# Operand addresses at multiples of 64 bytes, one expert instead of two read by columns, and a held decoding step

## The chip, the cores and the metric

The kernel runs on one core of a Trainium2 chip. The metric is the device time of one execution in microseconds (us); lower is better. The core has five engines: PE (TensorE, matrix products), DVE (VectorE), ACT (ScalarE), POOL (GpSimd) and SP (SyncE, which here issues most DMAs). Each works through its own queue in order. PEld is the loading of a matmul's stationary operand, which overlaps the matmul before it.

## The reference, cut to what matters

Three layers in a chain, all float32 inputs except that the last layer's weights come as 64-bit floats:

```python
# attention: batch 4, heads 12, sequence 448, head size 64
q_n, k_n = rmsnorm(q, g_q), rmsnorm(k, g_k)
attn = softmax(q_n @ k_n.T / 8)
x = (attn @ v)                       # -> [1792 tokens, 768]
# soft mixture of experts: 8 experts with 4 slots each
logits = x @ phi                     # [1792, 32]
slot_input = softmax(logits, over tokens).T @ x
slot_out[e] = relu(slot_input[e] @ w1[e]) @ w2[e]   # w1 768x1024, w2 1024x768
x = softmax(logits, over slots) @ slot_out
# feed forward
h = x @ w_in                         # 768 x 2048
g = h * sigmoid(1.702 * h)
out = g @ w_out                      # 2048 x 768
```

## The kernel before, in words

The work stands in three stretches of the span.

**Attention** (0 to about 300 us) runs over 24 pairs of heads with f16 scores; all engines take part. Its queues are written by a planner: each step is recorded with an engine, a cost, a due time and its needs, and `run()` sorts the steps of each engine into one order. The table `HOLD` adds needs to named steps.

**The experts** (about 300 to 394 us). 48 MB of expert weights stream in on SP's queue in a fixed order. For expert e, `first_half` (L1186) multiplies the slots by w1, `hidden_turn` (L1214 to L1218) transposes the hidden values through PE, and `second_half` (L1225) multiplies them by w2, whose rows arrive in pieces of 768 KB. For the last two experts (`EL = NE - 2`) w2 is not read in rows but in columns: `piece()` (L120) reads 512 or 256 of the 768 columns of 512 rows at a time, so that the last sums can start before all of it is there. Those sums are the planner's steps ("p", kk, ee): for each of six column blocks kk, `last_mm` (L1318) adds eight small matmuls of each of the two experts; ("pc", kk) copies the block on DVE (L1326), ("pt", kk) turns it on PE (L1329), ("pa", kk) adds it to `before` on DVE (L1333), and `u_step` (L1347) multiplies `before` by the first columns of w_in. While PE has nothing to do, `warm_c` (L1340) issues idle f16 matmuls into a spare tile. When all six blocks are summed, ACT copies u (L1693, called u0 below), PE makes the first hidden columns (`f_first`, L1430), ACT applies the activation (`f_hi` L1448, gh), and the first matmul into y (L1484) can run. `close()` then frees the buffers of the stage.

**The feed forward** (394 us to the end). w_out is 64-bit floats, loaded raw (`raw_w`, L1278) and decoded by ACT and DVE in steps (`decode64`, L167 to L181; steps ("wd", f, i, h)); `w_hi` (L1297, L1289) and `w_lo` (L1301) split each value into two fp32r tiles, wh and wl (named wo while they stand in one pool). The rest of w_in is loaded by `late_load` (L1369) and decoded likewise. The first 512 tokens go through `y_first` (L1484), 16 blocks f of 128 hidden columns each, three passes (hi x hi, hi x lo, lo x hi) of matmuls with 512 and 256 columns. The other 1,280 tokens go through `s_mm` (L1637): seven products instead of eight of half-size blocks, each again in three passes, every matmul a 128x128 stationary block of activations (gh, gl, sl) and 256 moving columns of weights (wo, wh, wl) or of sums of weights (th, tl), all fp32r. `f_mm` for these tokens is L1556.

**Addresses.** Tiles are laid out one after another in each of 128 partitions. The tile esc, [128, 1], takes 32 bytes and stands ahead of the large tiles on the left side; on the right side nothing stands ahead of them. By the address map of the built program the following operands of PE start at 32 bytes past a multiple of 64: lg, pacc, all of attention's rings, the weight rings wr, cT, gh, gl, gg, the ring of hs and pc, uh, ul, selu, keep, and the pairs of wo. These start at a multiple of 64: ident, wt, wi, the last eight wh and wl, th, tl, sg, sl, ust, hTz, siT and before. Of the matmuls of L1637 so 480 (wo by gh or gl, 440, and wo by sl, 40, where sl starts at a multiple) have a moving operand at 32, 741 (wh, wl, th or tl by gh or gl) have the moving operand at a multiple and the stationary one at 32, and 108 (th or wh by sl) have both at a multiple.

Of the kernel before, what the change touches and what calls it, by code (L numbers as in the profile page):

```python
# [8 lines left out]
F32 = mybir.dt.float32  # L9
# [5 lines left out]
ALU = mybir.AluOpType  # L15
# [5 lines left out]
def soft_moe_block_kernel(  # L21
# [60 lines left out]
    selw = const.tile([128, NS], F32, name="selw")  # L82
    gmax = const.tile([128, 1], F32, name="gmax")
    rgmax = const.tile([128, 1], F32, name="rgmax")
    esc = const.tile([128, 1], F32, name="esc")
    lg_t = const.tile([128, B, C, NS], F32, name="lg")
    pacc = const.tile([128, DM], F32, name="pacc")
    macc = [const.tile([128, 1], F32, name=f"macc{b}") for b in range(B)]
    zacc = const.tile([128, 1], F32, name="zacc")

    wpool_ctx = tc.tile_pool(name="wpool", bufs=NW, reuse_waits="tile")
    wpool = wpool_ctx.__enter__()

    EL = NE - 2
    order_w = [(x, e) for e in range(3) for x in ("w1", "w2")] + [("w1", 3)]
    order_w += [(x, e + d) for e in range(3, EL) for x, d in (("w1", 1), ("w2", 0))] + [("w1", NE - 1)]
    stream = [(x, e, hh) for x, e in order_w for hh in range(2)] + [("w2", EL, i) for i in range(4)]
    wt = {}  # L100
    is_kept = {}
    win64 = w_in.bitcast(U32)
# [3 lines left out]
    def place(t, kept=False, i=None, merged=False):  # L106

        if i is None:
            i = nstream[0]
            nstream[0] += 1  # L110
        kind, e, hh = key = stream[i]
        wt[key], is_kept[key] = t, kept

        def piece(n):
            if kind == "w1":
                rows = w1[e, hh * 384:hh * 384 + 384, :].rearrange("(p n) f -> p n f", n=3)
                nc.sync.dma_start(out=t[:, n * F1:(n + 1) * F1], in_=rows[:, n])
            elif e == EL:
                a, c = (0, 512, DM)[n:n + 2]
                nc.sync.dma_start(  # L120
                    out=t[:, 4 * a:4 * c].rearrange("p (f c) -> p f c", f=4),
                    in_=w2[EL + hh // 2, hh % 2 * 512:hh % 2 * 512 + 512, a:c].rearrange("(f p) c -> p f c", p=128),
                )
            else:
                r = hh * 512 + n // 2 * 256
                rows = w2[e, r:r + 256, :].rearrange("(p n) c -> p n c", n=2)
                nc.sync.dma_start(out=t[:, n * DM:(n + 1) * DM], in_=rows[:, n % 2])

        def whole(n):
            if kind == "w1":  # L130
                nc.sync.dma_start(out=t, in_=w1[e, hh * 384:hh * 384 + 384, :].rearrange("(p n) f -> p (n f)", n=3))
            else:
                r = hh * 512 + n * 256
                nc.sync.dma_start(
                    out=t[:, 2 * n * DM:2 * (n + 1) * DM], in_=w2[e, r:r + 256, :].rearrange("(p n) c -> p (n c)", n=2)
                )

        if merged and (kind == "w1" or e < EL):
            return [lambda n=n: whole(n) for n in range(1 if kind == "w1" else 2)]
        return [lambda n=n: piece(n) for n in range(3 if kind == "w1" else 4 if e < EL else 2)]  # L140

    late = []

    def load_all(t, kept=False):
        last = stream[nstream[0]][:2] == ("w2", EL)
        fs = place(t, kept, merged=True)
        if last:

            late.append(fs.pop())
        if len(late) == 4:  # L150
            fs += late
        for f in fs:
            f()

    def reload(*key):

        if is_kept[key] is not None and nstream[0] < len(stream) - (0 if is_kept[key] else 4):
            load_all(wt[key], is_kept[key])

    def decode64(dst, src, low):  # L160
# [82 lines left out]
    for i, tag in enumerate(("ssq", "y0", "nt")):  # L243
# [36 lines left out]
    HOLD = {  # L280
        ("meansq", 1): [("invert", 0, 5)], ("gain", 2): [("kn", 0)], ("square", 3): [("khi", 0)], ("q2", 0): [("khi", 0)],
        ("meansq", 2): [("qn", 0)], ("meansq", 3): [("qlo", 0)], ("lq", 1): [("v", 0)], ("e1", 2): [("tqb", 22)], ("ev", 0): [("tqb", 22)], ("ev", 1): [("tqb", 22)], ("v", 0): [("lq2", 0), ("lk2", 0)],
    }

    SHIFT = dict(
# [34 lines left out]
    def op(name, eng, dur, due, fn, needs=(), takes=None, gives=()):  # L320
        names[name] = len(ops)
        due += SHIFT.get(name if isinstance(name, str) else name[0], 0)
        ops.append((name, eng, dur, due, fn, list(needs) + HOLD.get(name, []), takes, list(gives)))
# [529 lines left out]
    def rtile(nm, shape, dt=F32):  # L853
        R[nm] = rt_p.tile(shape, dt, tag=nm, name=nm)
        return R[nm]
# [85 lines left out]
        nc.vector.tensor_copy(out=rtile("nmg", [128, 1]), in_=MS.pop("w"))  # L941

    def w_exp():
        nc.scalar.activation(out=rtile("wgt", [128, 1]), in_=macc[B - 1], func=AF.Exp, bias=R["nmg"], scale=1.0)

    def w_z():
        nc.vector.tensor_tensor(out=rtile("zs", [128, 1]), in0=R["wgt"], in1=zacc, op=ALU.mult)

    def w_sum():
        fill(9)  # L950
# [8 lines left out]
        nc.vector.reciprocal(out=rz, in_=R["zt"])  # L959

    def w_scale():
        nc.vector.tensor_scalar(out=selw, in0=sel32, scalar1=R["wgt"], scalar2=None, op0=ALU.mult)

    op("w_sel", "DVE", 0.2, 100, w_sel, [("exp", 4, 0, 0)])
    w_last = None
# [61 lines left out]
    with tc.manual_schedule():  # L1027
# [93 lines left out]
        def combine():  # L1121
            nm = bp.tile([P, B, C, 1], F32, name="nm")
            flat = lambda t: t.rearrange("p b c o -> p (b c o)")
            nc.vector.tensor_reduce(out=flat(nm), in_=lg_t.rearrange("p b c s -> p (b c) s"), axis=AX.X, op=ALU.max)
            nc.vector.tensor_tensor(out=lg_t, in0=lg_t, in1=nm.to_broadcast([P, B, C, NS]), op=ALU.subtract)
            nc.scalar.activation(out=lg_t, in_=lg_t, func=AF.Exp)
            nc.vector.tensor_reduce(out=flat(nm), in_=lg_t.rearrange("p b c s -> p (b c) s"), axis=AX.X, op=ALU.add)
            nc.vector.tensor_scalar(out=nm, in0=nm, scalar1=1e-9, scalar2=None, op0=ALU.add)
            rc = bp.tile([P, B, C, 1], F32, name="rc")
            nc.vector.reciprocal(out=flat(rc), in_=flat(nm))  # L1130
            nc.scalar.activation(out=bp.tile([128, 1], F32, name="warm"), in_=flat(rc)[:, :1], func=AF.Silu)
            nc.vector.tensor_tensor(out=lg_t, in0=lg_t, in1=rc.to_broadcast([P, B, C, NS]), op=ALU.mult)

        def combine_turn(b):
# [103 lines left out]
        for e in range(EL):  # L1238
# [1 line left out]
            hidden_turn(e)  # L1240
            first_half(e + 1, 1)
            second_half(e)
        first_half(NE - 1, 0)
        hidden_turn(EL)
        first_half(NE - 1, 1)
        sums_read()
        hidden_turn(NE - 1)
        while turns_w[1] < NWI:
            win_turn()
        w2ctx.close()  # L1250
# [57 lines left out]
            nc.scalar.activation(out=out, in_=ps[:, :3], func=AF.Copy)  # L1308
            nc.scalar.activation(out=dst[:, SF:], in_=ps[:, 3, :SH], func=AF.Copy)

        def last_mm(kk, ee):

            if ee == 0:
                st["p", kk] = ps_h.tile([128, Q1], F32, tag="h", name="h")
            for f in range(8):
                g, a, c = f % 4, *((0, 512) if kk < 4 else (512, DM))
                w = wt["w2", EL, 2 * ee + f // 4][:, 4 * a:4 * c].rearrange("p (f c) -> p f c", f=4)
                nc.tensor.matmul(  # L1318
                    st["p", kk][32 * g:32 * g + 32, :128], hTz[(EL + ee) % 2][:, f % 2, f // 2],
                    w[:, g, kk * 128 - a:kk * 128 - a + 128],  # L1320
                    start=(ee == 0 and f < 4), stop=(ee == 1 and f >= 4),
                )

        def last_copy(kk):
            st["pc", kk] = hp.tile([128, Q1], F32, tag="hs", name="pc")
            nc.vector.tensor_copy(out=st["pc", kk][:, :128], in_=st["p", kk][:, :128])  # L1326
# [346 lines left out]
        for i in range(60):  # L1673
            op(("warm", i), "PE", 0.11, IDLE, warm_c, [("warm", i - 1)] if i else [])
        for kk in range(KD):
            for ee in range(2):
                i = 2 * kk + ee
                if i < 8:
                    op(("arrive", i), "SP", (2.6 if i < 4 else 1.5) if i else 0, -1, lambda: None, [("arrive", i - 1)] if i else [])
                op(  # L1680
                    ("p", kk, ee), "PE", 0.62, kk, lambda kk=kk, ee=ee: last_mm(kk, ee),
                    [("arrive", kk // 4 * 4 + 2 * ee + 1)] + [("p", kk, 0)] * ee, None if ee else ("h", kk),
                )
            op(("pc", kk), "DVE", 0.22, kk, lambda kk=kk: last_copy(kk), [("p", kk, 1)], ("hs", kk), [("h", kk)])
            op(("pt", kk), "PE", 0.14, kk, lambda kk=kk: last_turn(kk), [("pc", kk)], None, [("hs", kk)])
            op(("pa", kk), "DVE", 0.09, kk, lambda kk=kk: last_add(kk), [("pt", kk)])
            op(
                ("u", kk), "PE", 0.5, kk + 2, lambda kk=kk: u_step(kk), [("pa", kk)] + ([("u", kk - 1)] if kk else []) + [("p", KD - 1, 1)] * (kk == KD - 2),
            )
        for b in range(B):  # L1690
            op(("cT", b), "ACT", 0.48, 1, lambda b=b: ct_copy(b))
# [32 lines left out]
        for f in range(KF):  # L1724
# [3 lines left out]
            for h in (None,) if f else (0, 1):  # L1728
                o = lambda *n, h=h: (n[0], f) + n[1:] + (() if h is None else (h,))
                n = 1 if h is None else 0.52  # L1730
                op(
                    o("raw"), "SP", 0.15 if h == 0 else 2.2 * n, f, lambda f=f, h=h: raw_w(f, h), [o("raw", h=0)] if h else [("arrive", 7)] if f < 3 else ["close"],
                    None if h else ("wr", f),
                )
                op(
# [184 lines left out]
```

## Time and profile before

| | us |
|---|---|
| median of 3 runs | 650.08 |
| lowest, highest | 648.41, 651.06 |
| the profiled execution's own time | 648.1 |
| its span in the profile | 646.3 |
| PE busy | 596.4 (92%) |
| DVE busy | 485.2 (75%) |
| ACT busy | 386.5 (60%) |

The profiled execution is 1.8 us longer than its span and 2.0 us below the median. Busy time on PE is modelled from its start times, since matmuls overlap: a matmul's duration (281 ns for 256 columns) is its passage, while the distance from one start to the next tells the rate. Shares are means over stretches with different limits, so the rows that count are those of one stretch.

### The profile page before, as it was taken

How to read it: one execution, taken by the hardware profiler on the slowest of the kernel's cores; microseconds unless marked ns; L12 is line 12 of the kernel's file. 1: busy time of each engine (PE TensorE's matmuls, PEld its weight loads, DVE VectorE, ACT ScalarE, POOL GpSimd, SP SyncE). 2: the span in 40 equal slices, each digit the busy share in tenths (PEclk: the TensorE clock that was granted, in tenths of full speed). 3: DMA queues.
4: the chain of work that ended last, by engine and by line, in shares of the span. 5: the costliest groups of instructions: out<-in, count | busy, mean ns of one | idle time of the engine just before them, and what ended most of it. 6: DMA issues, size and time to landing. Idle time of an engine off the chain costs nothing.

```text
span 646.3 us, 12124 instructions
## 1 busy us (share of the span) xinstructions
PE 596.4 (92%) x4575; PEld 399.4 (62%) x4575; DVE 485.2 (75%) x896; ACT 386.5 (60%) x768; POOL 170.3 (26%) x209
## 2 busy tenths in 40 slices
PE   2699999999999999999895788999999999999997
PEld 1333444344433443456452355887899999999997
DVE  6888979999999998546353118999999988565653
ACT  3767888877877786643333018998664545444442
POOL 3676683736774765120002000000000000000000
PEclk9999999999999999998999799999999999999999
DMA  7889999799999998956999997985120101010101
GB/s 188 294 166 225 215 190 174 168 232 208 188 222 200 179 237 202 282 190 249 409 415 419 413 374 279 333 282 192 41 97 3 50 1 50 2 50 1 51 2 50
DMA packets 143339, 121.55 MB, mean 188 GB/s; under 512 B 105232, under 2 KB 125968, under 8 KB 142000
## 3 DMA queue, kind: packets, MB, share of 16 engines
q1 hardware_dynamic: 141776, 116.41, 64.6%
q10 hardware_dynamic: 1440, 4.26, 1.7%
q8 instruction: 36, 0.59, 0.4%
q14 instruction: 23, 0.19, 0.1%
q0 software_dynamic: 64, 0.10, 0.1%
HBM read 92.18 MB, written 5.51 MB: 151 GB/s over the span
## 4 chain that ended last, share of the span: by engine, by line
PE 56%; DMA 13%; DVE 12%; ACT 7%; SPq 5%; issue 4%; POOL 2%; ACTq 0%; DVEq 0%; POOLq 0%
PE y L1637 24%; PE pv L597 5%; PE sc L578 5%; PE y L1484 5%; DVE wr L567 4%; DMA wr<-wr 3%; PE h L1186 3%; SPq L120 3%; DMA wt<-in_moe_w_dram 3%; DMA ws<-in_moe_w_in_dram 3%; DMA wr<-in_k_dram 2%; PE pv L592 2%; PE mx L562 2%; PE so_ps L1225 2%; PE f L1556 1%
## 5 line engine op out<-in xcount | busy, mean ns | idle before, releaser
L567 DVE TENSOR_REDUCE wr<-mx 128x2 f16<-128x896 f32 x92 | 99.9, 1086 | 15.9 <-PE mx L562 15.4
L582 ACT ACTIVATE e<-sc,esc 128x448 f32<-128x448 f32 x96 | 57.2, 633 | 8.2 <-PE sc L578 6.3
L1637 PE MATMUL y<-wo,gh 128*128 128x256 f32 x320 | 59.6, 281 | 0.0
L1582 ACT ACTIVATE gh<-gg 128x512 fp32r<-128x512 f32 x40 | 25.3, 631 | 56.8 <-PE y L1637 53.6
L585 POOL TENSOR_TENSOR es<-es,e 128x448 f32<-128x448 f32 x37 | 44.6, 1210 | 32.9 <-PE pv L597 22.0
L1588 DVE TENSOR_TENSOR gl<-gg,gh 128x512 fp32r<-128x512 f32 x40 | 27.6, 690 | 32.5 <-ACT gh L1582 32.3
L578 PE MATMUL sc<-wr 128*128 128x448 f16 (+1 forms) x192 | 47.6, 360 | 2.4 <-ACT e L582 2.2
L1637 PEld LDWEIGHTS y<-wo,gh 128*128 128x128 f32 x320 | 49.2, 190 | 0.0
L1637 PE MATMUL y<-wl,gh 128*128 128x256 f32 x172 | 48.4, 281 | 0.0
L1637 PE MATMUL y<-wh,gh 128*128 128x256 f32 x172 | 48.3, 281 | 0.0
L582 ACT ACTIVATE es<-sc,esc 128x448 f32<-128x448 f32 x54 | 33.5, 635 | 20.3 <-PE sc L578 20.1
L445 ACT ACTIVATE wr<-wr 128x512 f32<-128x512 f32 x48 | 30.2, 635 | 15.3 <-DVE wr L1056 4.5
L1637 PE MATMUL y<-wh,gl 128*128 128x256 f32 x138 | 38.8, 281 | 0.0
L578 PEld LDWEIGHTS <-wr 128*128 128x128 f16 (+1 forms) x256 | 19.1, 101 | 30.2 <-issue 21.6
L1563 ACT ACTIVATE gg<-f 128x512 f32<-128x512 f32 x40 | 23.8, 599 | 16.8 <-DVE gl L1588 13.8
L1637 PE MATMUL y<-wo,gl 128*128 128x256 f32 x120 | 33.9, 282 | 0.0
L450 DVE TENSOR_REDUCE wr<-wr 128x16 f32<-128x1024 f32 x24 | 29.1, 1211 | 5.7 <-ACT wr L445 5.7
L505 POOL TENSOR_TENSOR wr<-wr 128x512 f32<-128x512 f32 x26 | 30.2, 1180 | 11.8 <-DVE wr L498 7.5
L1637 PEld LDWEIGHTS y<-wh,gh 128*128 128x128 f32 x172 | 32.4, 188 | 0.0
L1637 PEld LDWEIGHTS y<-wl,gh 128*128 128x128 f32 x172 | 32.4, 188 | 0.0
L1637 PE MATMUL y<-tl,gh 128*128 128x256 f32 x111 | 31.2, 281 | 0.0
L1637 PE MATMUL y<-th,gh 128*128 128x256 f32 x111 | 31.2, 281 | 0.0
(325 smaller groups left out, 1673.4 us busy)
## 6 DMA issues: line engine op xcount, KB each, us to landing
wt<-in_moe_w_dram SPq DMA_DIRECT2D x9, 1536.0 KB, 10.2
wr<-in_moe_w_out_dram SPq DMA_DIRECT2D x15, 768.0 KB, 6.3
wt<-in_moe_w_dram SPq DMA_DIRECT2D x12, 512.0 KB, 7.8
wr<-in_moe_w_dram SPq DMA_DIRECT2D x8, 768.0 KB, 12.3
ws<-in_moe_w_in_dram SPq DMA_DIRECT2D x12, 512.0 KB, 4.8
wr<-in_moe_w_dram SPq DMA_DIRECT2D x12, 384.0 KB, 5.5
out_dram<-o SPq DMA_DIRECT2D x12, 384.0 KB, 2.4
wr<-in_k_dram SPq DMA_DIRECT2D x11, 384.0 KB, 5.3
```

The source lines that it names most:

```text
L445: nc.scalar.activation(out=sqt[p][:, 8 * i:8 * i + 8], in_=rows(p, i), func=AF.Square, scale=D ** -0.5)
L450: nc.vector.tensor_reduce(out=part(ssqt, p, 1), in_=sqt.pop(p), axis=AX.X, op=ALU.add)
L505: eng.tensor_tensor(out=n, in0=n, in1=r.to_broadcast([P, 8, D]), op=ALU.mult)
L567: nc.vector.tensor_reduce(out=lanes(of(qb_t, p), 1)[:m, h:h + n, c, 0:1], in_=MX.pop((p, g))[:m, :n, :S], axis=AX.X, op=ALU.max,)
L578: nc.tensor.matmul(out, cols(a, n, c), cols(b, n), start=first, stop=not first)
L582: nc.scalar.activation(out=E[p, h, c], in_=SC.pop((p, h, c)), func=AF.Exp, scale=esc)
L585: on(f"e{h}{c}", p)[0].tensor_tensor(out=E[p, h, 0], in0=E[p, h, 0], in1=E[p, h, c], op=ALU.add)
L597: nc.tensor.matmul(PV[p][h * D:(h + 1) * D, :], t[:, 6 * n + 3 * h + c], E[p, h, c], start=(c == 0), stop=False)
L1484: nc.tensor.matmul(Y[t, u], a[:, t * 128:(t + 1) * 128], b[:, YC[u]], start=(f == 0 and j == 0 and (u == 0 or t % 2 == 0)), stop=(f == KF ...
L1582: nc.scalar.activation(out=t, in_=src, func=AF.Copy)
L1588: nc.vector.tensor_tensor(out=t, in0=src, in1=hi.bitcast(F32), op=ALU.subtract)
L1637: nc.tensor.matmul(out, l[:, a], r, start=fresh and x == 0, stop=last and x == 2)
```

## The change

Three edits.

1. Addresses. esc moves behind the large tiles of its pool; a new pool of 32 bytes on the right edge holds wgt (before in a ring) and so moves every pool on the right by 32 bytes; a one-column tile called warm is dropped. By the address map of the changed program the operands of PE start at multiples of 64 bytes, but for sub-slices inside a few small tiles (one column of macc, the strides of selw, pacc and hs).
2. `EL = NE - 1`: only expert 7's w2 is read by columns, in two pieces of 1 MB and two of 0.5 MB. Expert 6's w2 is read in four pieces of rows and multiplied in `second_half`. A step ("p", kk) has 8 matmuls instead of 16.
3. `HOLD` makes the first decoding steps of w_out on DVE, ("wd", 0, 0, 0) and ("wd", 0, 0, 1), wait for ("pa", 5), the last sum.

```diff
@@ the tiles
-    esc = const.tile([128, 1], F32, name="esc")
     lg_t = const.tile([128, B, C, NS], F32, name="lg")
...
     zacc = const.tile([128, 1], F32, name="zacc")
+    esc = const.tile([128, 1], F32, name="esc")
+    edge = ctx.enter_context(tc.tile_pool(name="edge", bufs=1, side="right"))
+    wgt = edge.tile([128, 1], F32, name="wgt")
...
-            nc.scalar.activation(out=bp.tile([128, 1], F32, name="warm"), in_=flat(rc)[:, :1], func=AF.Silu)
+            nc.scalar.activation(out=macc[0], in_=flat(rc)[:, :1], func=AF.Silu)
@@ the last experts
-    EL = NE - 2
+    EL = NE - 1
...
-    order_w += [(x, e + d) for e in range(3, EL) for x, d in (("w1", 1), ("w2", 0))] + [("w1", NE - 1)]
-    stream = [(x, e, hh) for x, e in order_w for hh in range(2)] + [("w2", EL, i) for i in range(4)]
+    order_w += [(x, e + d) for e in range(3, EL) for x, d in (("w1", 1), ("w2", 0))]
+    stream = [(x, e, hh) for x, e in order_w for hh in range(2)] + [("w2", EL, i) for i in range(2)]
...
-                    in_=w2[EL + hh // 2, hh % 2 * 512:hh % 2 * 512 + 512, a:c].rearrange("(f p) c -> p f c", p=128),
+                    in_=w2[EL, hh * 512:hh * 512 + 512, a:c].rearrange("(f p) c -> p f c", p=128),
...
-        first_half(NE - 1, 0)
         hidden_turn(EL)
-        first_half(NE - 1, 1)
         sums_read()
-        hidden_turn(NE - 1)
...
-                    st["p", kk][32 * g:32 * g + 32, :128], hTz[(EL + ee) % 2][:, f % 2, f // 2],
+                    st["p", kk][32 * g:32 * g + 32, :128], hTz[EL % 2][:, f % 2, f // 2],
                     w[:, g, kk * 128 - a:kk * 128 - a + 128],
-                    start=(ee == 0 and f < 4), stop=(ee == 1 and f >= 4),
+                    start=(f < 4), stop=(f >= 4),
@@ the held step
     HOLD = {
...
+        ("wd", 0, 0, 0): [("pa", 5)], ("wd", 0, 0, 1): [("pa", 5)],
     }
```

The planner writes new orders from this. On DVE, at the end of the experts, the queue before (pc is a copied block of the last sums, before+= its sum, wf and wr tiles of the decoding of w_out, keep a copy of before):

```order
L1326 COPY pc<-h 128x128
L181 TENSOR_SCALAR wf<-wf 128x384
L1326 COPY pc<-h 128x128
L1333 TENSOR_TENSOR before<-t,before 128x32
L181 TENSOR_SCALAR wf<-wf 128x384
L1333 TENSOR_TENSOR before<-t,before 128x32
L167 SCALAR_TENSOR_TENSOR wf<-wr,wf 128x384 x4
L1722 COPY keep<-before 128x192
L1301 TENSOR_TENSOR wo<-wf,wo 128x384 x2
L167 SCALAR_TENSOR_TENSOR wr<-wr 128x768
```

and in the changed program (its line numbers differ by a few):

```order
L1324 COPY pc<-h 128x128
L1331 TENSOR_TENSOR before<-t,before 128x32 x2
L183 TENSOR_SCALAR wf<-wf 128x384 x2
L169 SCALAR_TENSOR_TENSOR wf<-wr,wf 128x384 x4
L1715 COPY keep<-before 128x192
L169 SCALAR_TENSOR_TENSOR wr<-wr 128x768
L1301 TENSOR_TENSOR wo<-wf,wo 128x384 x2
L169 SCALAR_TENSOR_TENSOR wf<-wf,wr 128x768
```

The two TENSOR_SCALARs moved behind the last sum, and the STT of f = 1 (wr by wr) ahead of the two subtractions of f = 0.

On ACT, at the same place, the queue before (wf by wr is the first step of a block's decoding, wr by wr the second, u the copy u0, wo the splitting, gh and gg the activation of the first hidden columns):

```order
L170 ACTIVATE wf<-wr 128x384 x2
L170 ACTIVATE wf<-wr 128x768
L1693 ACTIVATE u_3945<-u 32x256
L1297 ACTIVATE wo<-wf 128x384
L1289 ACTIVATE wo<-wf 128x384
L173 ACTIVATE wr<-wr 128x768
L1448 ACTIVATE gh<-h 128x512
L1443 ACTIVATE gg<-h 128x512
```

and in the changed program:

```order
L172 ACTIVATE wf<-wr 128x384 x2
L172 ACTIVATE wf<-wr 128x768
L175 ACTIVATE wr<-wr 128x768
L1686 ACTIVATE u_3971<-u 32x256
L1297 ACTIVATE wo<-wf 128x384
L1289 ACTIVATE wo<-wf 128x384
L172 ACTIVATE wf<-wr 128x768
L1446 ACTIVATE gh<-h 128x512
```

The second step of f = 1, wr by wr, moved ahead of u0, and the first step of f = 2 ahead of gh.

On PE, the last expert's hidden values and the sums before (h by wt,siT is L1186, so_ps `second_half`, h by wt,hTz or wr,hTz the last sums):

```order
L1186 MATMUL h<-wt,siT 32x256 x12
L1225 MATMUL so_ps<-wr,hTz_3356 32x256 x24
L1186 MATMUL h<-wt,siT 32x256 x12
L1214 MATMUL t<-ident,hs 128x128 x2
L1186 MATMUL h<-wt,siT 32x256 x12
L1207 MATMUL t<-ident,so 128x96 x2
L1214 MATMUL t<-ident,hs 128x128 x2
```

and in the changed program:

```order
L1189 MATMUL h<-wt,siT 32x256 x12
L1228 MATMUL so_ps<-wr,hTz_3359 32x256 x24
L1189 MATMUL h<-wt,siT 32x256 x12
L1217 MATMUL t<-ident,hs 128x128 x2
L1189 MATMUL h<-wt,siT 32x256 x12
L1228 MATMUL so_ps<-wt,hTz_3358 32x256 x24
L1217 MATMUL t<-ident,hs 128x128 x2
L1210 MATMUL t<-ident,so 128x96 x2
```

Expert 6's 24 matmuls by rows of w2 are new there. Behind these rows the idle matmuls go from 37 to 15, and the last sums from 96 matmuls to 48.

## Rows read from the trace of the kernel before

**Rows 1.** The page: busy time of each engine; chain that ended last, by line.

```profile
PE 596.4 (92%) x4575; PEld 399.4 (62%) x4575; DVE 485.2 (75%) x896; ACT 386.5 (60%) x768; POOL 170.3 (26%) x209
...
PE y L1637 24%; PE pv L597 5%; PE sc L578 5%; PE y L1484 5%; DVE wr L567 4%; DMA wr<-wr 3%; PE h L1186 3%; SPq L120 3%; DMA wt<-in_moe_w_dram 3%; DMA ws<-in_moe_w_in_dram 3%; DMA wr<-in_k_dram 2%; PE pv L592 2%; PE mx L562 2%; PE so_ps L1225 2%; PE f L1556 1%
```

**Rows 2.** Stretches: start:end, length, busy (count) of PE, PEld, DVE, ACT, POOL, clock, DMA.

```profile
448.20:642.24 194.04, 194.01 (x1569) 190.34 (x1565) 147.09 (x352) 96.78 (x171) 0.00 (x0) 1.00 0.09 34
...
394.70:420.00 25.30, 23.59 (x130) 20.09 (x131) 24.62 (x35) 24.26 (x39) 0.00 (x0) 1.00 0.92 326
420.00:448.20 28.20, 27.29 (x234) 23.19 (x233) 26.67 (x37) 26.19 (x42) 0.00 (x0) 1.00 0.70 240
```

**Rows 3.** Timeline of PE, a stretch with wo moving (start, us, line, tiles, count).

```profile
552.76 0.40 PE L1637 MATMUL y<-wo,gh 128*128 128x256 f32 x2
...
553.84 0.28 PE L1637 MATMUL y<-th,gh 128*128 128x256 f32 x1
```

**Rows 4.** The same, a stretch with th, tl, wh and wl moving.

```profile
541.64 0.28 PE L1637 MATMUL y<-th,gh 128*128 128x256 f32 x1
...
541.88 0.28 PE L1637 MATMUL y<-th,sl 128*128 128x256 f32 x1
...
543.76 0.40 PE L1637 MATMUL y<-wo,gh 128*128 128x256 f32 x2
```

**Rows 5.** Timeline of PE, f16 matmuls: idle ones on ident, and attention's scores.

```profile
373.85 1.80 PE L1340 MATMUL t<-ident 128*128 128x256 f16 x15 [0.28 <-DVE hTz L1218]
...
100.79 1.31 PE L578 MATMUL sc<-wr 128*128 128x448 f16 x6
```

**Rows 6.** Groups of PE from 448.2 to 642.24, shapes apart (count, busy, mean ns).

```profile
L1637 PE MATMUL y<-wo,gh 128*128 128x256 f32 x320 | 59.6, 281 | 0.0
...
L1484 PE MATMUL y<-wh,gh 128*128 128x512 f32 x24 | 6.6, 398 | 0.0
```

**Rows 7.** Timeline of all engines around the last sum and the first y.

```profile
389.05 0.36 DVE L181 TENSOR_SCALAR wf<-wf 128x384 uint32<-128x384 uint32 x1 [0.65 <-ACT wf L170]
...
390.10 1.93 PE L1347 MATMUL u<-wi,before 128*32 128x256 f32 x32
...
391.38 0.95 ACT L170 ACTIVATE wf<-wr 128x768 f32<-128x768 f32 x1 [1.40 <-DMA wr<-in_moe_w_out_dram]
...
392.22 0.37 ACT L1693 ACTIVATE u<-u 32x256 f32<-32x256 f32 x1
...
392.64 1.98 PE L1430 MATMUL h<-c,u 32*128 32x512 f32 x4
...
393.31 0.91 ACT L173 ACTIVATE wr<-wr 128x768 uint32<-128x768 uint32 x1
...
394.74 0.73 PE L1484 MATMUL y<-wo,gh 128*128 128x512 f32 x2
```

**Rows 8.** Stretches: w2 in rows; then columns of 1 MB; then of 0.5 MB.

```profile
357.60:363.44 5.84, 4.63 (x48) 1.84 (x40) 0.53 (x2) 0.00 (x0) 0.00 (x0) 0.77 1.03 422
370.72:381.54 10.82, 7.70 (x101) 5.08 (x101) 1.01 (x5) 2.75 (x9) 0.00 (x0) 1.00 1.05 381
381.54:387.47 5.93, 5.85 (x140) 4.55 (x144) 1.93 (x8) 0.00 (x0) 0.00 (x0) 1.00 1.09 362
```

**Rows 9.** Timeline of PE, a wait for a producer in the first 512 tokens.

```profile
442.34 1.68 PE L1484 MATMUL y<-wh,gh 128*128 128x512 f32 x8 [0.75 <-ACT wh L1297]
```

**Rows 10.** Stretches in which the granted clock fell among the experts.

```profile
354.00:360.00 6.00, 4.61 (x38) 1.94 (x39) 2.10 (x5) 1.20 (x2) 0.00 (x0) 0.50 1.01 414
...
366.00:370.00 4.00, 2.88 (x25) 1.29 (x26) 0.00 (x0) 0.00 (x0) 0.00 (x0) 0.63 0.98 400
```

**Rows 11.** Timeline of PE: waits for expert weights, and `first_half` at two clocks.

```profile
367.12 2.79 PE L1186 MATMUL h<-wt,siT 128*32 128x256 f32 x24 [2.58 <-DMA wt<-in_moe_w_dram]
...
370.76 1.50 PE L1186 MATMUL h<-wt,siT 128*32 128x256 f32 x24 [0.24 <-DMA wt<-in_moe_w_dram]
...
381.58 0.43 PE L1318 MATMUL h<-wr,hTz 128*32 128x128 f32 x8 [2.12 <-DMA wr<-in_moe_w_dram]
```

More of the change, by code (lines that the diff above doesn't have):

```diff
@@ L149, in load_all @@
             late.append(fs.pop())
-        if len(late) == 4:
+        if len(late) == 2:
             fs += late
@@ L155, in reload @@
     def reload(*key):
-        if is_kept[key] is not None and nstream[0] < len(stream) - (0 if is_kept[key] else 4):
+        if is_kept[key] is not None and nstream[0] < len(stream) - (0 if is_kept[key] else 2):
             load_all(wt[key], is_kept[key])
@@ L943, in w_exp @@
     def w_exp():
-        nc.scalar.activation(out=rtile("wgt", [128, 1]), in_=macc[B - 1], func=AF.Exp, bias=R["nmg"], scale=1.0)
+        nc.scalar.activation(out=wgt, in_=macc[B - 1], func=AF.Exp, bias=R["nmg"], scale=1.0)
     def w_z():
-        nc.vector.tensor_tensor(out=rtile("zs", [128, 1]), in0=R["wgt"], in1=zacc, op=ALU.mult)
+        nc.vector.tensor_tensor(out=rtile("zs", [128, 1]), in0=wgt, in1=zacc, op=ALU.mult)
     def w_sum():
@@ L961, in w_scale @@
     def w_scale():
-        nc.vector.tensor_scalar(out=selw, in0=sel32, scalar1=R["wgt"], scalar2=None, op0=ALU.mult)
+        nc.vector.tensor_scalar(out=selw, in0=sel32, scalar1=wgt, scalar2=None, op0=ALU.mult)
     op("w_sel", "DVE", 0.2, 100, w_sel, [("exp", 4, 0, 0)])
@@ L1309, in ct_copy, with last_mm @@
             nc.scalar.activation(out=dst[:, SF:], in_=ps[:, 3, :SH], func=AF.Copy)
-        def last_mm(kk, ee):
-            if ee == 0:
-                st["p", kk] = ps_h.tile([128, Q1], F32, tag="h", name="h")
+        def last_mm(kk):
+            st["p", kk] = ps_h.tile([128, Q1], F32, tag="h", name="h")
             for f in range(8):
                 g, a, c = f % 4, *((0, 512) if kk < 4 else (512, DM))
-                w = wt["w2", EL, 2 * ee + f // 4][:, 4 * a:4 * c].rearrange("p (f c) -> p f c", f=4)
+                w = wt["w2", EL, f // 4][:, 4 * a:4 * c].rearrange("p (f c) -> p f c", f=4)
                 nc.tensor.matmul(
-                    st["p", kk][32 * g:32 * g + 32, :128], hTz[(EL + ee) % 2][:, f % 2, f // 2],
+                    st["p", kk][32 * g:32 * g + 32, :128], hTz[EL % 2][:, f % 2, f // 2],
                     w[:, g, kk * 128 - a:kk * 128 - a + 128],
-                    start=(ee == 0 and f < 4), stop=(ee == 1 and f >= 4),
+                    start=(f < 4), stop=(f >= 4),
                 )
@@ L1675, in soft_moe_block_kernel @@
         for kk in range(KD):
[L1676 to L1684, printed above, removed]
+            if kk < 4:
+                op(("arrive", kk), "SP", (2.6 if kk < 2 else 1.5) if kk else 0, -1, lambda: None, [("arrive", kk - 1)] if kk else [])
+            op(("p", kk), "PE", 0.62, kk, lambda kk=kk: last_mm(kk), [("arrive", kk // 4 * 2 + 1)], ("h", kk))
+            op(("pc", kk), "DVE", 0.22, kk, lambda kk=kk: last_copy(kk), [("p", kk)], ("hs", kk), [("h", kk)])
             op(("pt", kk), "PE", 0.14, kk, lambda kk=kk: last_turn(kk), [("pc", kk)], None, [("hs", kk)])
@@ L1687, in soft_moe_block_kernel @@
             op(
-                ("u", kk), "PE", 0.5, kk + 2, lambda kk=kk: u_step(kk), [("pa", kk)] + ([("u", kk - 1)] if kk else []) + [("p", KD - 1, 1)] * (kk == KD - 2),
+                ("u", kk), "PE", 0.5, kk + 2, lambda kk=kk: u_step(kk), [("pa", kk)] + ([("u", kk - 1)] if kk else []) + [("p", KD - 1)] * (kk == KD - 2),
             )
@@ L1731, in soft_moe_block_kernel @@
                 op(
-                    o("raw"), "SP", 0.15 if h == 0 else 2.2 * n, f, lambda f=f, h=h: raw_w(f, h), [o("raw", h=0)] if h else [("arrive", 7)] if f < 3 else ["close"],
+                    o("raw"), "SP", 0.15 if h == 0 else 2.2 * n, f, lambda f=f, h=h: raw_w(f, h), [o("raw", h=0)] if h else [("arrive", 3)] if f < 3 else ["close"],
                     None if h else ("wr", f),
```

## The prediction, made before the changed kernel was run

> **What bounds the kernel now.** I read the page first: PE is busy 92% of the span [rows 1], a mean over three stages. The windows by stretch say more [rows 2]. From 448.2 to 642.24 PE is busy 194.01 of 194.04 us at clock 1.00, while DVE has 47 us to spare and ACT 97: this stretch, 30% of the span, is pure PE, and only the distance between matmuls can shorten it. From 394.7 to 448.2 DVE is busy 51.29 and ACT 50.45 of 53.5 us: there the decoding of w_out sets the pace. PE waits for it, as at 442.34, 0.75 us for a wh just written [rows 9]. The stretch of the experts goes with the DMAs, at 362 to 422 GB/s [rows 8]. Attention, before it, has its own paragraph below.
>
> Next I looked at the distance between fp32r matmuls. With wo moving and gh or gl stationary, both at 32 past a multiple of 64, nine starts lie in 553.84 - 552.76 = 1.08 us: 120.0 ns each [rows 3]. With moving operands at a multiple, and a few of the stationary ones (sl) too, 18 starts take 543.76 - 541.64 = 2.12 us: 117.8 ns [rows 4]. Idle f16 matmuls of the same 256 columns, both operands at a multiple, take (1.80 - 0.27) / 14 = 109 ns, 0.27 being the passage of the last [rows 5]. So alignment may matter, but these rows differ in type too: attention's f16 scores, at 32, take (1.31 - 0.36) / 5 = 190 ns for 448 columns, the same 0.425 ns per column as the aligned f16 [rows 5].
>
> **The change part by part.**
>
> Addresses. The stretch of pure PE holds 1,569 recorded matmuls [rows 2], nearly all of 256 columns like the first row of [rows 6]; L1484's of 512 (the second row, for each of three passes: 72) count twice. That makes 1,641 units of 256 columns, 194.04 / 1,641 = 118.2 ns each. With every operand at a multiple of 64 the unit lies between 118.2 (nothing gained) and 109.1 (the aligned f16 row): 0 to 1,641 x 9.1 ns = 14.9 us. No row shows a long run with both operands aligned. Aligning the moving one is worth 2.2 ns where it shows (120.0 to 117.8), and the few sl's there say little by themselves. I take the middle, 113.65, since no row is nearer to either end: 1,641 x 4.55 ns = **-7.5 us**. It is on the path entirely, since PE never waits here. Would DVE and ACT keep up? DVE is busy 147 of the then 186 us, ACT 97 [rows 2]. The y of the first 512 tokens before 448.2 gain nothing: their producers set the pace.
>
> The Trainium skill ("SBUF — State Buffer", Specifications) gives lines of 16 bytes and full bandwidth from two hits on a line. By that rule an operand at 32 already starts on a line, and the sum would lack the 7.5 us. The 120.0 against 117.8 ns speak mildly against it.
>
> Attention. Its f16 scores run at the f16 rate already [rows 5], so I put it at nothing; its products with v (pv, 5% and 2% of the chain [rows 1], 45 us) have no row that tells their distance: bounds 0 and, at the same 3.8%, -1.7 us; I take 0, as for the scores.
>
> Expert 6 by rows. Columns came at 381 (1 MB) and 362 GB/s (0.5 MB), rows at 422 [rows 8]. Expert 6's 3.1 MB take 2.1 / 0.381 + 1.05 / 0.362 = 8.4 us before, at 422 GB/s 7.45. Since the 381 stretch also holds rows, I take -0.7 us for the last landing (0.1 to 1.0). Its 24 products by rows lie in time in which PE waits for DMA (as before 367.12 and 381.58 [rows 11]): nothing. The 48 last-sum matmuls that go save some 0.3 us behind the landing.
>
> HOLD. One TENSOR_SCALAR, at 389.05 (0.36 us) [rows 7], stands ahead of the copy of the last block in DVE's queue, the other between the last two sums: about 0.3 us each. In all the last sum comes 0.7 + 0.3 + 0.6 = 1.6 us sooner; PE's u, which ended at 390.10 + 1.93 = 392.03, then ends near 390.4.
>
> But u0 on ACT cannot follow. Ahead of it stands the decoding of f = 1, waiting for its raw block (391.38, 0.95 us), and now also wr by wr (0.91) [rows 7]. With the raw block 0.7 sooner: 390.7 + 0.95 + 0.91 = 392.55, against 392.22 for u0 before. Then come 1.98 us of f (392.64) and the activation, and the first y stays near 394.74 although the sum is ready earlier. What is won is that step itself: 0.9 us of ACT's work is done ahead, and the STT of f = 1 that follows it on DVE is ahead likewise. In the stretch to 448.2, which these two engines limit, I count **-0.9 us**. Bounds: -2 (all of the 1.6 and the pieces of order come through) and +2.5 (the new order of late steps makes PE wait three more times as at 442.34).
>
> Sum: -7.5 - 0.9 = -8.4. The profiled execution took 648.1 (span 646.3 and 1.8 around it), so it would take 639.7; it lay 2.0 under the median 650.08, on whose scale I predict **641.7**.
>
> **The rivals.** Each with its time.
>
> Partly, my forecast: the unit falls to between 112 and 117 ns, giving about -11 to -3 us with the tail; centre 641.7.
>
> Full rate: with both operands aligned fp32r runs at the f16 row's 109.1 ns. For: the plateau of exactly 120.0 looks like a fixed addition per matmul, and the stationary operand was at 32 in nearly all rows. Against: the aligned moving operand alone brought little. 650.1 - 14.9 - 0.9 = **634.3**. The Trainium skill ("TensorE: Matmul & The Clock Gate", "Wait — 56ns, not 53.3ns?") has a distance of columns / 2.4 GHz plus 2.5 ns; by that, as an estimate, 256 columns take 109.2 ns, as the f16 row does, but fp32r at 118 to 120 does not.
>
> Nothing from addresses: fp32r is slow by its type, and 117.8 against 120.0 has another cause. For: f16 does not care [rows 5]. Then only the tail is left: **649.2**, which can't be told from no change.
>
> Slower: the clock at the last sums. PE's granted clock was 0.50, the level of 1.2 GHz, from 354 to 360, and 0.63 in the mean from 366 to 370 [rows 10], there behind a wait of 2.58 us; 24 matmuls of `first_half` then took 2.79 instead of 1.50 us [rows 11]. After a wait of 2.12 before 381.58 it did not fall, with 37 idle matmuls ahead of it. Now 15 are left, and expert 6's rows come in bursts. If the clock is half from the last sums to the first y's, then by 2.79 / 1.50 u's last 24 matmuls (of 32 in 1.93 us) go from 1.45 to 2.7, f from 1.98 to 3.7, and y's for as long as the 6 us of [rows 10] lose 3: +6.0, less the 1.6 and 0.9 won: +3.5, and with nothing from addresses **653.6**. It decides from 2.5 us lost on, and only without the alignment's gain. Against: the clock was 1.00 from 370.72 to 381.54, where PE is busy 7.70 of 10.82 us [rows 8].
>
> **How the numbers follow.** Partly 0.60, full rate 0.20, nothing 0.15, slower 0.05. 0.5% of 650.08, about what a measurement can tell from no change, is 3.25 us: 646.8 and 653.3. Partly and full rate are faster, 0.80; nothing is the same, 0.15; slower 0.05. The range takes in half of full rate and half of nothing, and leaves out 0.10 + 0.07 + 0.05: **634.3 to 649.2**.
>
> **What would show it.** In the changed profile: the timeline of PE with wo, gh should have starts under 117 ns apart, all classes alike, and the stretch from the first wait-free y to the last should be 186 to 187 us. The part before 448 should hardly change: last expert weights about 0.7 us earlier, pc5 with no TENSOR_SCALAR ahead, u's end near 390.4, u0 no earlier than 392. I am wrong if the fp32r distance stays at 118 to 120 (then the addresses do nothing), if it falls to 109, or if the clock row at 380 to 396 is under 1.00 and y starts after 396.

## The result, and the profile after

The changed kernel takes 654.99 us in the median of 13 runs (650.26 to 657.32), the kernel before 650.08 in as many (648.35 to 652.79). The ratio is 1.0065, with a 95% interval of 1.0045 to 1.0085: slower by 0.65%, where 641.7 was predicted. The profiled execution of the changed kernel is its shortest, 650.26 us, with a span of 648.5, so its trace shows less of the loss than most executions have.

The page of the changed kernel, busy time by engine and the chain by line:

```profile
PE 596.6 (92%) x4505; PEld 399.2 (62%) x4505; DVE 486.1 (75%) x896; ACT 386.5 (60%) x768; POOL 169.2 (26%) x209
...
PE y L1635 25%; PE sc L581 8%; PE pv L600 8%; DMA wst<-in_moe_w_in_dram 4%; PE y L1482 4%; PE mx L565 3%; PE pv L595 3%; DMA ws<-in_moe_w_in_dram 3%; DMA wt<-in_moe_w_dram 2%; DMA wr<-in_moe_w_dram 2%; SPq L122 2%; DVE wr L570 2%; DMA wr<-in_moe_w_out_dram 2%; PE f L1554 1%; PE ms L612 1%
```

Against [rows 1] the page says little: the busy times are the same within 1.1 us, and the chain has y first with 25% instead of 24%, but takes another way through attention and the DMAs. The place has to come from the stretches, here those of the changed kernel from its first y on (columns as in [rows 2]):

```profile
392.52:420.00 27.48, 25.23 (x141) 21.74 (x142) 24.76 (x35) 25.14 (x40) 0.00 (x0) 1.00 0.85 306
420.00:448.20 28.20, 27.84 (x198) 23.85 (x197) 27.15 (x38) 26.26 (x42) 0.00 (x0) 1.00 0.82 273
448.20:480.00 31.80, 30.23 (x224) 26.33 (x224) 30.31 (x56) 21.89 (x36) 0.00 (x0) 1.00 0.11 41
480.00:640.00 160.00, 160.00 (x1336) 160.00 (x1335) 112.39 (x289) 73.34 (x133) 0.00 (x0) 1.00 0.07 26
```

PE starts its first y 2.2 us sooner than before (392.52 against 394.74 in [rows 7]), and DVE and ACT have more idle time up to 420. PE still waits after 448.20, where before it was full [rows 2]. Behind 480 it is full in both; there the distance tells. Timeline of PE in the changed kernel, the same pieces of work as [rows 3] and, further down, [rows 4]:

```profile
552.82 0.40 PE L1635 MATMUL y<-wo,gh 128*128 128x256 f32 x2
...
553.90 0.28 PE L1635 MATMUL y<-wo,gh 128*128 128x256 f32 x1
```

```profile
542.02 0.28 PE L1635 MATMUL y<-th,gh 128*128 128x256 f32 x1
...
542.26 0.28 PE L1635 MATMUL y<-th,sl 128*128 128x256 f32 x1
...
544.06 0.28 PE L1635 MATMUL y<-th,gl 128*128 128x256 f32 x1
544.18 0.40 PE L1554 MATMUL f<-cT,ust 128*128 128x256 f32 x2
```

With wo nine starts lie in 1.08 us, 120.0 ns as before. With wh, wl, th and tl the 18 starts from 542.02 to 544.18 take 2.16 us, 120.0 ns, where [rows 4] has 117.8. Aligning everything made the faster part as slow as the slower one. The tile's own view of the changed kernel (duration in ns: least, median, greatest; first and last start) shows how regular that is:

```profile
L1635 PE MATMUL y<-wo,gh x320: 283/283/283, 489.8 to 627.6; 128*128 128x256 f32 x160
L1635 PE MATMUL y<-wh,gh x172: 283/283/283, 476.6 to 643.9; 128*128 128x256 f32 x172
```

Last the place between, around u0 and the first y, in the timeline of the changed kernel:

```profile
387.46 0.62 DVE L183 TENSOR_SCALAR wf<-wf 128x384 uint32<-128x384 uint32 x2
...
388.33 0.96 ACT L172 ACTIVATE wf<-wr 128x768 f32<-128x768 f32 x1 [1.39 <-DMA wr<-in_moe_w_out_dram]
389.19 0.91 ACT L175 ACTIVATE wr<-wr 128x768 uint32<-128x768 uint32 x1
...
390.00 0.36 ACT L1686 ACTIVATE u<-u 32x256 f32<-32x256 f32 x1
...
392.52 2.37 PEld L1482 LDWEIGHTS y<-wo,gh 128*128 128x128 f32 x12 [0.96 <-ACT gh L1446]
```

As foretold, u0 waits behind wr by wr. But all of it is earlier, partly because attention itself ended 1.4 us earlier in this execution. So from here on every trace is cut at its own events, with differences of start times of PE: the last matmul of the slots' input (selw by pacc, "attention"), the first y, the first matmul with sl, the last y. From the last y to the end all traces have 4.3 to 4.9 us.

Each column after the first counts from the event before it. "U0 first" and "places apart" are explained with the experiments.

| kernel | attention ends at | to first y | to first sl | to last y |
|---|---|---|---|---|
| before | 301.47 | 93.27 | 97.26 | 149.92 |
| changed | 300.08 | 92.44 | 99.35 | 152.28 |
| changed, profiled again | 304.23 | 92.48 | 102.28 | 152.28 |
| addresses only | 300.54 | 93.54 | 99.07 | 152.28 |
| without the addresses | 303.50 | 93.22 | 102.24 | 149.92 |
| without the held step | 303.11 | 92.62 | 102.26 | 152.28 |
| changed, stationary at 32 | 299.20 | 93.48 | 101.72 | 149.36 |
| before, places apart | 299.68 | 93.56 | 98.05 | 149.35 |
| before, moving at 32 | 301.62 | 93.72 | 98.41 | 150.25 |
| before, moving at 16 | 301.17 | 92.52 | 98.67 | 150.50 |
| changed, u0 first | 300.73 | 92.21 | 99.70 | 152.28 |
| u0 first, places apart | 300.93 | 92.73 | 97.39 | 149.35 |
| the same, no held step | 301.65 | 92.07 | 97.07 | 149.35 |

The last column belongs to the addresses. The one before it belongs mainly to the order, but each row is one execution, and traces with one and the same order still differ there by up to 3 us (99.35 and 102.28 for the changed kernel, 97.26 to 99.07 for the order of before). The first is noise: the same kernel ended attention at 300.08 and at 304.23. The second scatters by about 1 us in either order.

### The profile page after: what moved, and what is told of

It reads as the page before. It is cut to its first block, busy times and chain, and to the rows that moved or that the text cites. A ratio compares the mean times of both kernels' runs of the same rounds, so it can differ in the third digit from the quotient of the medians.

```text
span 648.5 us, 11990 instructions
## 1 busy us (share of the span) xinstructions
PE 596.6 (92%) x4505; PEld 399.2 (62%) x4505; DVE 486.1 (75%) x896; ACT 386.5 (60%) x768; POOL 169.2 (26%) x209
## 4 chain that ended last, share of the span: by engine, by line
PE 60%; DMA 15%; DVE 9%; ACT 7%; SPq 4%; issue 3%; POOL 2%; ACTq 0%; POOLq 0%; DVEq 0%
PE y L1635 25%; PE sc L581 8%; PE pv L600 8%; DMA wst<-in_moe_w_in_dram 4%; PE y L1482 4%; PE mx L565 3%; PE pv L595 3%; DMA ws<-in_moe_w_in_dram 3%; DMA wt<-in_moe_w_dram 2%; DMA wr<-in_moe_w_dram 2%; SPq L122 2%; DVE wr L570 2%; DMA wr<-in_moe_w_out_dram 2%; PE f L1554 1%; PE ms L612 1%
```

## The experiments

**Addresses only.** The first edit alone, on the kernel before:

```diff
-    esc = const.tile([128, 1], F32, name="esc")
...
+    esc = const.tile([128, 1], F32, name="esc")
+    edge = ctx.enter_context(tc.tile_pool(name="edge", bufs=1, side="right"))
+    wgt = edge.tile([128, 1], F32, name="wgt")
```

> Only the addresses of the change, on the kernel before; experts and held step as before. Theory A (with stationary and moving operand at the same place in 64 bytes the fp32r stretch settles at a constant 120.0 ns instead of a scattered 118): starts at 120.0 ns throughout from about 480 us on, pure-PE stretch some 3 us longer, time 653 to 655. Rival B (the extra time comes from the new order behind the experts): within 1 us of the kernel before. Rival C (addresses help, the order costs more): faster than before.

653.43 us against 650.47, ratio 1.0042 (1.0018 to 1.0067). The tile's view of this run:

```profile
L1639 PE MATMUL y<-wo,gh x320: 283/283/283, 491.1 to 628.9; 128*128 128x256 f32 x160
L1639 PE MATMUL y<-wh,gh x172: 283/283/283, 477.9 to 645.2; 128*128 128x256 f32 x172
```

All 1,396 distances between 256-column matmuls from the first L1639 on are 120 ns; in the kernel before they average 118.2 with a spread of 2.2. There, 474 have a moving operand at 32 and the next matmul's stationary operand at 32 too, and they average 118.3. So 120.0 is not the price of one pair of addresses but a steady beat, kept where every pair is at the same place; pairs at different places break it, for their neighbours too. Theory A held, with one limit: by the address map, the operands of this stretch coincide in 512 bytes, not only in 64, so that 64 is not shown to be the size that counts.

**Without the addresses.** The changed kernel with esc and wgt back where they were:

> The change without its addresses: one expert by columns and the held step stay, esc and wgt stand where they stood. Theory A: starts at a scattered 118 ns as before, first y some 1 to 2 us earlier, time 648.5 to 650.5. Rival B: as slow as the changed kernel, 654 to 656.

652.40 us, ratio 1.0029 (1.0002 to 1.0055): between the two theories. The beat is gone (149.92), but the stretch from the first y to the first sl grew by 5 us. (The profiled execution, 655.07 us, is the longest of the twelve; by the medians 1.9 us are lost.) So there are two costs, of which theory A knew one.

**Stationary operands at 32.** The changed kernel, its addresses kept but for three pads:

```diff
+        poolf("pad_a", 1, side="right").tile([128, 1], F32, name="pad_a")
         cp = {t: poolf(t + "_p", FB[t], side="right") for t in ("gl", "gh", "gg")}
+        poolf("pad_b", 1, side="right").tile([128, 1], F32, name="pad_b")
...
             for t in ("sg", "sl"):
                 cp[t] = poolf(t + "_q", FB[t])
+                poolf("pad_" + t, 1).tile([128, 1], F32, name="pad_" + t)
```

(one pad behind sg, one behind sl, so that th and tl stay at a multiple).

> The changed kernel with three pads of 32 bytes that put the stationary operands gh, gl and sl at 32 past a multiple of 64 while all moving operands stay at multiples. Theory A (it is the equal place that locks the distance): no plateau of 120.0, mean at or under 118, time 1.5 to 4 us under the changed kernel's 655. Rival D (what counts is that the moving operand, wo above all, left 32): the plateau of 120.0 stays and the time is that of the changed kernel.

649.90 us, ratio 0.9994 (0.9970 to 1.0018), some 5 us under the changed kernel where 1.5 to 4 were expected; the stretch to the last y is 149.36, 2.9 us under that of the addresses alone. All 1,396 distances average 117.6 ns, the 1,328 between operands at different places 117.4; the other 68, before a matmul of hidden columns (cT by ust, both still at a multiple), 122. The moving operands of y stand where they stood, so rival D falls. Whether the stationary operands' own place counts or their place relative to the moving ones, this run can't tell; the one with the places the other way round does.

**Without the held step.** The changed kernel without the `HOLD` entry of the change:

> The changed kernel without the held step. Theory A: the same plateau of 120.0; the last sum some 0.6 us later, u0 on ACT unchanged behind the raw block; time within 1 us of the changed kernel. Rival B (the held step's new order is what costs): 3 to 5 us faster than the changed kernel.

654.31 us, ratio 1.0056 (1.0025 to 1.0086), the changed kernel's own figure. The first y is 0.2 us later behind attention, less than that column scatters. The held step neither costs nor brings anything that shows. In the built programs its queues are those of the changed kernel but for a few places on DVE, so the rest of the new order comes from the second edit.

**Before, with the places apart; the places the other way round; and a step of 16.** Three runs on the order of before. In the first, the addresses of the change and the pads; in the second a pad of 32 bytes ahead of each pool with a moving operand instead; in the third the tiles of wh, wl, th and tl are cut 16 bytes into their slots:

```diff
-                wh[f], wl[f] = (cp["wo"].tile([128, DM], F32R, name=f"w{x}{f}") for x in "hl")
+                wh[f], wl[f] = (cp["wo"].tile([128, DM + 8], F32R, name=f"w{x}{f}")[:, 4:DM + 4] for x in "hl")
```

> The kernel before (two experts by columns, no held step) with the addresses of the change and the three pads that put gh, gl and sl at 32 while every moving operand is at a multiple of 64: no pair at the same place. Theory A: the stretch from the first sl to the last y at 149.4 us as with the changed experts (149.36 there, 149.92 before, 152.28 with the addresses of the change alone), the first 512 tokens in 97 to 99 us since the order is that of before; time 649 to 650, 3 to 4 us under the addresses alone. Rival: the order of before brings nothing, 102 us for the first 512 tokens.

> The kernel before with the places the other way round: every moving operand at 32 past a multiple of 64, every stationary one at a multiple. Theory A (only the places relative to each other count): 149.4 us from the first sl to the last y, mean 117.5 ns, time 649 to 650. Rival D (the moving operand's own place counts): 152 us or another figure.

> The kernel before with the addresses of the change, but wh, wl, th and tl of the last eight blocks moved to 16 or 48 past a multiple of 64, wo and the stationary operands at multiples. If the places count in steps of 16 or less: stretches with wh and wl leave 120.0, to somewhere between 109 and 118, those with wo may stay at 120.0; the stretch 149 to 151 us. If only a difference of 32 counts: 120.0 throughout. If an odd 16 costs an access more: over 120 for these.

Measured: 648.72 us, ratio 0.9985 (0.9959 to 1.0011); 650.33, 0.9989 (0.9963 to 1.0016); 649.74, 0.9997 (0.9972 to 1.0022). None can be told from the kernel before. Their traces can: 149.35, 150.25 and 150.50 us to the last y, all without the beat. With the stationary operands at multiples and the moving ones at 32 the beat is gone as well, so it is the two places together that make it. The tile's view of the first of them:

```profile
L1642 PE MATMUL y<-wo,gh x320: 277/280/283, 489.3 to 624.4; 128*128 128x256 f32 x160
L1642 PE MATMUL y<-wh,gh x172: 277/279/282, 476.5 to 640.4; 128*128 128x256 f32 x172
```

Every difference that was tried breaks the beat, 16 bytes too (118.0 to 118.3 ns for wh, wl, th and tl there, and 119.0 for the 548 pairs left at the same place). But the exchange is not quite symmetrical: 117.6 ns with the moving operands at a multiple, 118.5 with the stationary ones, 150.25 us where theory A had 149.4. The pads also set the operands apart by other amounts in 512 bytes: in the run with the places the other way round the 580 pairs that are 32 bytes apart average 117.5 ns, 479 that are 96 apart 119.6. In the two runs with gh, gl and sl at 32, the 32 or 33 pairs that are 64 apart (th, then ust) take 125 to 127 ns, though 64 is no difference in 64 bytes. So more than the place in 64 bytes seems to count; no run separates it. Nothing came near the 109 ns of f16 [rows 5].

**The order.** The traces with the changed order share a pattern behind the first y. Waits of PE in the second profile of the changed kernel (its first y at 396.71):

```profile
418.93 1.66 PE L1482 MATMUL y<-wo,gh 128*128 128x512 f32 x8 [1.60 <-ACT wo L1297]
449.53 1.66 PE L1482 MATMUL y<-wh,gh 128*128 128x512 f32 x8 [1.68 <-ACT wh L1297]
461.78 0.73 PE L1433 MATMUL f<-cT,ust 128*128 128x512 f32 x2 [1.10 <-DVE ust L1421]
462.97 0.49 PE L1433 MATMUL f<-cT,ust 128*128 128x512 f32 x1 [0.45 <-ACT gg L1441]
463.63 2.47 PE L1482 MATMUL y<-wh,gh 128*128 128x512 f32 x8 [0.17 <-ACT gh L1450]
```

and the stretches around the last of them (columns as in [rows 2]):

```profile
456.00:460.00 4.00, 4.00 (x52) 3.46 (x44) 3.93 (x6) 2.49 (x4) 0.00 (x0) 1.00 0.00 0
460.00:464.00 4.00, 2.28 (x12) 1.35 (x11) 3.94 (x6) 3.43 (x6) 0.00 (x0) 1.00 0.00 0
464.00:468.00 4.00, 4.00 (x15) 3.34 (x14) 4.00 (x6) 3.73 (x7) 0.00 (x0) 0.57 0.02 4
468.00:472.00 4.00, 4.00 (x25) 3.51 (x24) 3.59 (x7) 0.85 (x1) 0.00 (x0) 1.00 0.00 0
```

The decoders come late with a wo, a wh and an ust; behind the last of these waits, with PE busy 2.28 of 4 us, the granted clock falls to a mean of 0.57, near its lower level of 1.2 GHz, and 15 matmuls pass in a stretch that takes 25 in the next. Four of the five traces with the changed order have such a fall behind the first y, all but the first profile of the changed kernel; none of the eight with another order has one there. PE's waits of 0.2 us and more ahead of the first sl add up to 5.5 to 5.8 us in these four, to 4.0 in the first profile, and to 1.7 to 4.6 in the eight. Queue SP in the same run, and what it had ahead of the late pieces of w_in (ws):

```profile
396.65 0.80 SPq L1367 DMA_DIRECT2D ws<-in_moe_w_in_dram  x2
397.51 1.61 SPq L1278 DMA_DIRECT2D wr<-in_moe_w_out_dram  x3
404.98 2.17 SPq L1367 DMA_DIRECT2D ws<-in_moe_w_in_dram  x2
407.20 4.27 SPq L1278 DMA_DIRECT2D wr<-in_moe_w_out_dram  x2
```

The third ws is issued 8.3 us behind the first y, where the kernel before had it after 6.7. I had let this queue pass as unchanged in its work. To give it its turns back I added needs: raw blocks of w_out behind late pieces of w_in, and u0 ahead of the second step of f = 1 on ACT, with the pads kept ("u0 first, places apart" in the table).

```diff
+        ("raw", 5): [("lw", 2, 2)], ("raw", 6): [("lw", 2, 3)], ("raw", 7): [("lw", 2, 4)], ("raw", 8): [("lw", 2, 5)],
+        ("wd", 1, 0): ["u0"],
```

> The changed kernel with the pads, and with needs added that give the SP queue its turn-taking back (the raw blocks of w_out 5 to 8 wait for the third to sixth late piece of w_in) and put u0 ahead of the second step of f = 1 on ACT. If the paired loads behind the first y are what makes the first 512 tokens longer: 97 to 99 us there instead of 101.7, first y 92 to 92.5 us behind the end of attention, time 646.5 to 648.5. If it is something else in the order: 101 us or more, time as with the pads alone, 649 to 651.

648.76 us against 650.83, ratio 0.9961 (0.9939 to 0.9983): faster than both kernels, and 0.3 us over the range expected. The stretch to the first sl falls from 101.72 to 97.39. SP's queue of this run (first y at 393.66):

```profile
393.60 0.80 SPq L1371 DMA_DIRECT2D ws<-in_moe_w_in_dram  x2
394.45 0.92 SPq L1282 DMA_DIRECT2D wr<-in_moe_w_out_dram  x2
400.15 0.33 SPq L1371 DMA_DIRECT2D ws<-in_moe_w_in_dram  x1
400.52 0.43 SPq L1282 DMA_DIRECT2D wr<-in_moe_w_out_dram  x1
403.11 0.33 SPq L1371 DMA_DIRECT2D ws<-in_moe_w_in_dram  x1
```

and PE's last two waits in its first 512 tokens:

```profile
430.38 0.73 PE L1437 MATMUL f<-cT,ust 128*128 128x512 f32 x2 [1.00 <-ACT ust L1427]
441.61 1.67 PE L1486 MATMUL y<-wh,gh 128*128 128x512 f32 x8 [0.23 <-ACT wh L1301]
```

In the built programs the need of u0 alone gives this very order on every engine; the needs of the raw blocks add nothing to it. So one step on ACT, at its new place, had turned the planner's whole order behind it. That order as a whole is what costs, as the next run shows; whether SP's turns or the order of the decoders does most of it was not separated.

**The two costs apart.** The changed kernel with only the need of u0 (beat kept), and the faster run without the held step:

> The changed kernel, its addresses left as they are, with one need added: the second step of f = 1 on ACT waits for u0 (which alone gives every queue the order of the run with the order restored). If order and addresses are two separate costs: the first 512 tokens in 97.5 to 98.5 us, the stretch from the first sl to the last y still 152.28 at 120.0 ns, time 650.5 to 652.5, some 3 us under the changed kernel and 2.5 to 3 over the run with the order restored and the places apart.

> The run with the order restored and the places apart, without the held decoding step. If the held step is worth what its queue shows: the last sum and the first y up to 0.6 us later behind the end of attention (92.7 there), time 0 to 1 us longer than that run's 648.8. If it is worth nothing, the same within the measurement.

The first: 650.81 us, ratio 1.0010 (0.9988 to 1.0031). The beat is there, 152.28, and the time is as expected, though its first 512 tokens took 99.70, 1.2 more than I allowed: mainly two waits, 1.45 us at 409.86 and 1.40 at 442.85; the beat, which begins some 15 us ahead of the first sl, adds some 0.4 (15.24 us there against 14.84 with the places apart). Against the changed kernel, measured again in the same session (654.37, below), the one need is worth 3.6 us. By the medians the order costs less elsewhere: 1.9 us without the addresses (with expert 6 by rows in it), 1.5 between the run with the stationary operands at 32 and the one with the order restored, each against its own kernel before. The second: 646.92 us against 650.56, ratio 0.9954 (0.9933 to 0.9976), the fastest of all; the held step again brings nothing.

**The changed kernel again.**

> The changed kernel once more, since its profiled execution was the shortest of thirteen. If its other executions lose their time behind the first y, as the runs with its order but other addresses do: 101.5 to 103 us from the first y to the first sl instead of 99.35, with PE's clock under 1.00 after the waits at some 51 to 66 us behind the first y, and 152.28 behind it. If they lose it in attention: 99.4 us again, and the end of attention at 302 to 305 us.

654.37 us, ratio 1.0055 (1.0031 to 1.0079). Its profiled execution, 657.39 us, is the longest of its twelve. The trace has both in part: the first sl 102.28 us behind the first y with the clock's fall shown above, as expected from the first reading, and attention ending at 304.23, as from the second. The 99.35 us of the first profile, without a fall of the clock, were the exception among the five traces with the changed order (102.24, 102.26 and 101.72 in the other three, all with such a fall). Why the end of attention moves by 4 us between executions is open.

## Why the prediction was wrong

- **What bounds the kernel**: right. The last 150 us are pure PE, and only the distance changes them. The stretch to 448 goes by its decoders.
- **"Aligning the moving one is worth 2.2 ns where it shows"**: this is the step that failed. [Rows 3] and [rows 4] did hold the cause, but they differ in two things: moving operands at a multiple, and at another place than the stationary ones. I took the first for the cause. The run with the stationary operands at 32 has its moving operands in y at multiples like the run with the addresses alone, and 117.6 instead of 120.0 ns. So the term is +2.4 us in the pure stretch (152.28 - 149.92), some +3 in all (650.47 to 653.43, by the ratio's interval 1.2 to 4.4), instead of -7.5. The rule that the text set against the gain, lines of 16 bytes in the Trainium skill ("SBUF — State Buffer", Specifications), agrees with the runs in that putting every operand at a multiple of 64 gained nothing (152.28 us against 149.92); it says nothing of two operands at the same place, and by it alone the time would not have risen.
- **Bounds of that term**, "nothing gained" to the aligned f16 row: the upper one was argued from one side only. A plateau at exactly 120.0 was in [rows 3], and a state into which everything could fall was not among the rivals. A distance of 120 was named as a sign of being wrong, but read as "the addresses do nothing".
- **"Expert 6 by rows"** and the sum: right in kind. The last u starts 1.04 us earlier behind attention (89.15 against 90.19); 1.6 was predicted. Over the five traces of each order it is 0.7 us in the mean, with a scatter of 1 us in either.
- **"u0 on ACT cannot follow"**: u0 did stand behind wr by wr, but the raw block came 1.7 us sooner (88.25 against 89.91 behind attention), not 0.7, so the first y was 0.83 us earlier, not equal. The other four traces with the order of before have this block at 89.2 to 89.3, so about 1 us is the better figure.
- **"What is won is that step itself ... -0.9 us"**: wrong. The step ahead won nothing in the stretch to the first sl; the order that the planner made behind it cost 2 to 5 us there in the traces, 1.5 to 3.6 by the medians. The bound, "+2.5 (... three more waits)", named the place and was too small: four waits of 0.5 to 1.7 us, and the clock.
- **The slower rival** named the clock, at the last sums. There it was 1.00 throughout in both profiles of the changed kernel; in the second it fell 70 us later, behind the waits that the new order made. At the last sums it did fall in four other traces (means of 0.57 to 0.74 over 4 us, from 380 or 384 on), three of them with the 37 idle matmuls of before, so the 15 that are left do not decide it. Their first y comes at 92.7 to 93.7 us behind attention, 0.3 to 1.2 us later than in traces of the same order without a fall; the rival had +6.0.
- **The held step**: 0.6 us expected, nothing measured, with the changed order or the restored one.
- **Attention at nothing**: its end moves by 4 us without any edit, so a microsecond there can't be told.

Together, by the medians: addresses +3.0 (the run alone), the order and expert 6 by rows +1.9 (the run without the addresses), 4.9 against a measured 654.99 - 650.08 = 4.9. Each of these is uncertain by 1 to 2 us by its interval, so that they agree to a tenth is luck.

## What to carry to other kernels

Before crediting a gain to a property of one operand, look in the trace for what else differs in the two rows compared; here it was the place of one operand relative to the other, and a pad of 32 bytes decided it. A planner's order is part of every edit: read the queues that come behind the edited place, DMA queues first, and if one step has changed sides, hold it where it was and see whether the rest returns. Cut traces at their own events before comparing them, since one stretch (attention here) can move by more than the effect.

## What was not expected of the hardware

Fp32r matmuls of 256 columns at full clock fall into a beat of exactly 120 ns when the moving operand and the next matmul's stationary one always stand at the same place: 1,396 distances, every one 120, in the run with the addresses alone. In that program the places coincide in 512 bytes; whether 64 would be enough was not tried. With stationary operands moved by 32 bytes the distances scatter around 117.6 ns, with moving ones moved by 32 around 118.5, and with wh, wl, th and tl moved by 16 those average 118.2. Pairs at different places keep those at the same place from it: in the kernel before, 474 pairs at the same 32 averaged 118.3. In the first 512 tokens of the changed kernel, where matmuls of 512 and 256 columns alternate, the beat does not form although all operands are at multiples: 256 columns average 118.2 ns with a spread of 1.8. What in the chip makes it was not tried.
